# Sliding-window attention and a GELU MLP, two layers twice over: the written-out order of all queues replaced by another, with new engine choices and bank numbers

## The chip, the cores and the metric

The kernel runs on one core of a Trainium2 chip. The metric is the device time of one execution in microseconds, lower is better. The profile is one execution of the kernel before; its engines are PE (TensorE matmul, with its weight loads as PEld), DVE (VectorE), ACT (ScalarE), POOL (GpSimd) and SP (SyncE, which here issues every DMA).

## The reference

Four steps on x of shape 1 x 2048 x 512, bf16, each with a residual:

```python
x = x + _A_ref(_layernorm(x, axis=-1), A_wqkv, A_wo)
x = x + _B_ref(_layernorm(x, axis=-1), B_w1, B_b1, B_w2, B_b2)
x = x + _A_ref(_layernorm(x, axis=-1), A_wqkv, A_wo)
x = x + _B_ref(_layernorm(x, axis=-1), B_w1, B_b1, B_w2, B_b2)
```

A is attention with 32 heads of 16, each position seeing itself and the 255 positions before it, and an output projection. B is an MLP 512 to 1792 to 512 with a tanh GELU. The two layers use the same weights twice.

## The kernel before, in words

The 2048 positions are 16 tiles of 128, and the two repetitions make 32 tiles. Attention goes by blocks of two tiles: blocks 0 to 7 are the first repetition, 8 to 15 the second. The MLP goes by ten jobs of two or four tiles (jobs 0 to 9). What one repetition writes to X the next one reads, tile by tile, so that a block of the second repetition can start as soon as its tiles have left the MLP.

For each block: layernorm statistics on DVE (L591, L593), the power of -1/2 on POOL (L603, L609; L603 can also run on DVE), the normalized tile on DVE (L619), its transpose by DMA (L624), or on PE for tiles 0 to 3 of the first and the last two of the last MLP (L631, moved out of PSUM on DVE at L580 or on ACT at L582). Then the projections on PE (L645): Q moved out by DVE (L580) or ACT (L582), K by DVE with a parity mask (L679), V by DVE or ACT (L580, L582). A copy of V shifted by 64 partitions is made by two DMAs.

Scores come in "visits": ten per block, five in the first block of a repetition. One visit computes 512 columns for four head pairs into two pairs of PSUM banks (L746, 8 to 24 matmuls of 32 rows, four at a time side by side), then ACT takes the exponential of each pair of banks (L753, 128 x 1024, two per visit, 300 in all), and DVE or POOL multiplies the parts at the window's edge by a 0/1 mask (L774). After half of the visits, PE multiplies by V and a column of ones (L796, 64-row and 17-column pieces), DVE transposes the result (L805), takes the reciprocal of the sums (L809), DVE or POOL normalizes (L813), DVE transposes back (L819), PE projects (L645, Wo_sb) and DVE adds the residual (L841).

An MLP job runs 14 first products (L645, xnTB with W_sb); six of them are moved out by DVE with the bias (L863) and pass through GELU on ACT in pairs (L866), eight go straight through GELU on ACT (L871). The second product (L645, W_sb with gT) accumulates 14 matmuls per tile; POOL prepares X + b2 in advance (L879), DVE adds (L886), and in the second repetition SP writes the tile out (L890). The last tile's second product is done in two halves of 256 columns.

**What sets the order.** Every step is a node: a PE step (one to 128 matmuls), one instruction of DVE, ACT or POOL, or one DMA. There are 3097. Nothing is scheduled when the program is built: `_ORDER` is a list of all node numbers, and each engine executes its nodes in the order in which they stand there. `_ALT` lists the nodes that run on their second engine instead of their first, and `_BANKS` gives, in that same order, the first PSUM bank of each group that is opened. A recording layer (`_Sched.op`) then adds the semaphore waits that the data and the eight banks require.

```python
for i in _ALT:
    nodes[i]["eng"], nodes[i]["fn"] = nodes[i]["alts"][1]
...
for i in _ORDER:
    ...
    for g, k in nd["alloc"]:
        b = next(banks)
        gmap[g] = tuple(range(b, b + k))
```

PE has 18 warm-up matmuls on a tile of zeros (L531; seven of them with 32 columns instead of 512), which stand at the start of its queue, and one small transpose of the MLP's bias (L564), whose input comes by a DMA of its own.

Of the kernel before, what the change touches and what calls it, by code (L numbers as in the profile page):

```python
# [19 lines left out]
class _Sched:  # L20
# [147 lines left out]
    15, 34, 5, 0, 6, 14, 35, 7, 33, 28, 38, 29, 47, 8, 18, 23, 9, 36, 3, 26, 31, 10, 57, 37, 11, 22, 1, 40, 4, 24, 2,  # L168
    58, 59, 61, 17, 42, 62, 21, 60, 65, 41, 63, 19, 64, 68, 55, 32, 66, 107, 39, 69, 67, 20, 105, 50, 70, 48, 30, 27,
    53, 25, 106, 108, 71, 109, 49, 72, 110, 73, 16, 74, 114, 81, 75, 82, 111, 83, 84, 115, 85, 86, 116, 112, 87, 88,  # L170
    89, 113, 195, 153, 117, 127, 128, 151, 196, 129, 130, 154, 118, 152, 131, 119, 197, 155, 120, 156, 98, 99, 100,
    121, 12, 101, 90, 13, 102, 367, 91, 368, 104, 159, 92, 93, 157, 94, 103, 325, 76, 369, 199, 77, 326, 95, 78, 200,
    79, 370, 132, 80, 133, 96, 134, 135, 201, 323, 97, 203, 198, 137, 136, 158, 138, 205, 144, 139, 202, 140, 145,
    204, 141, 146, 160, 147, 122, 520, 217, 148, 123, 206, 124, 219, 143, 125, 208, 126, 46, 218, 324, 43, 213, 209,
    327, 328, 215, 166, 167, 168, 331, 169, 214, 207, 371, 176, 329, 177, 521, 373, 210, 178, 330, 216, 179, 522, 171,
    172, 180, 372, 161, 173, 211, 142, 174, 170, 56, 375, 220, 162, 376, 332, 163, 164, 523, 175, 524, 221, 374, 377,
    150, 212, 165, 149, 380, 378, 222, 188, 382, 189, 44, 190, 181, 45, 525, 182, 381, 223, 385, 183, 224, 191, 386,
    184, 384, 226, 225, 227, 54, 231, 232, 387, 379, 233, 526, 234, 383, 333, 228, 185, 343, 388, 389, 334, 192, 229,
    235, 344, 395, 194, 230, 335, 396, 345, 238, 346, 291, 390, 236, 397, 239, 237, 347, 240, 336, 241, 348, 337, 349,
    338, 242, 350, 244, 339, 243, 391, 399, 351, 401, 340, 341, 352, 400, 245, 403, 342, 392, 402, 51, 353, 405, 52,  # L180
    354, 355, 398, 356, 186, 360, 404, 357, 361, 362, 527, 363, 393, 408, 364, 253, 409, 260, 261, 407, 254, 262, 410,
    359, 413, 255, 246, 247, 415, 411, 256, 412, 257, 248, 249, 250, 258, 414, 406, 564, 251, 273, 394, 274, 566, 263,
    276, 416, 267, 268, 417, 565, 264, 270, 271, 265, 277, 642, 285, 286, 423, 567, 418, 640, 275, 643, 528, 287, 529,
    428, 272, 419, 282, 252, 283, 429, 288, 259, 289, 641, 420, 308, 290, 309, 421, 424, 266, 310, 311, 279, 278, 644,
    269, 422, 645, 284, 307, 280, 312, 281, 313, 314, 315, 540, 425, 426, 568, 427, 541, 570, 316, 648, 542, 543, 649,
    317, 569, 544, 318, 530, 531, 319, 532, 187, 533, 572, 534, 193, 320, 574, 321, 646, 430, 431, 322, 647, 292, 573,
    293, 294, 432, 577, 295, 435, 579, 366, 576, 296, 545, 297, 436, 358, 571, 298, 433, 578, 546, 582, 434, 547, 437,
    584, 548, 575, 550, 438, 899, 551, 552, 650, 583, 553, 439, 651, 441, 652, 440, 653, 554, 900, 897, 585, 592, 654,
    299, 549, 300, 301, 593, 365, 302, 303, 304, 442, 581, 305, 594, 586, 535, 536, 898, 580, 596, 537, 306, 598, 538,
    587, 901, 539, 902, 597, 595, 600, 588, 557, 601, 660, 661, 662, 663, 599, 602, 605, 664, 558, 559, 607, 560, 655,  # L190
    656, 561, 457, 458, 606, 603, 610, 903, 657, 589, 658, 612, 904, 604, 453, 590, 459, 454, 476, 455, 477, 611, 485,
    486, 563, 609, 479, 591, 480, 482, 562, 613, 659, 470, 471, 483, 556, 905, 464, 465, 467, 478, 468, 484, 608, 450,
    460, 469, 461, 906, 451, 466, 446, 452, 447, 481, 443, 487, 448, 444, 473, 472, 462, 665, 474, 456, 614, 666, 667,
    445, 463, 615, 449, 475, 616, 684, 625, 626, 668, 617, 489, 686, 620, 618, 490, 491, 492, 685, 493, 619, 621, 494,
    669, 688, 687, 627, 690, 628, 622, 629, 495, 488, 623, 689, 496, 632, 692, 497, 694, 498, 624, 691, 499, 500, 501,
    630, 502, 693, 697, 504, 631, 505, 633, 1017, 506, 698, 507, 508, 634, 509, 1018, 510, 503, 635, 699, 511, 702,
    1019, 670, 512, 704, 700, 671, 672, 1020, 695, 673, 1021, 703, 674, 712, 696, 513, 514, 701, 676, 714, 515, 706,
    516, 517, 705, 518, 713, 519, 716, 638, 707, 717, 715, 718, 833, 720, 708, 721, 677, 917, 1022, 918, 919, 709,
    722, 920, 719, 710, 725, 921, 678, 727, 679, 680, 724, 681, 726, 730, 922, 636, 923, 1023, 731, 912, 924, 728,
    1024, 913, 723, 914, 915, 732, 729, 925, 711, 941, 637, 943, 734, 907, 908, 909, 733, 910, 916, 926, 555, 735,  # L200
    942, 639, 1025, 911, 736, 945, 934, 946, 935, 675, 737, 947, 738, 683, 949, 1026, 936, 739, 948, 951, 937, 740,
    938, 741, 742, 682, 950, 743, 944, 954, 744, 745, 955, 746, 747, 750, 952, 748, 940, 927, 749, 956, 959, 953, 928,
    752, 929, 961, 930, 1037, 751, 1038, 753, 931, 1039, 754, 1040, 960, 755, 957, 969, 970, 756, 758, 757, 963, 971,
    973, 962, 1027, 1028, 1041, 974, 1029, 759, 1030, 1031, 958, 977, 978, 964, 975, 787, 965, 788, 979, 789, 976,
    790, 776, 782, 791, 982, 981, 777, 1274, 983, 778, 779, 972, 780, 984, 987, 980, 783, 784, 988, 785, 966, 986,
    765, 786, 766, 767, 985, 768, 989, 771, 769, 772, 773, 774, 991, 1061, 775, 1063, 990, 1065, 967, 1067, 992, 968,
    1062, 1276, 760, 761, 762, 1066, 993, 763, 803, 804, 805, 806, 1068, 1277, 764, 1069, 798, 1070, 994, 799, 800,
    1275, 995, 801, 818, 1071, 819, 820, 821, 1278, 808, 996, 849, 809, 810, 811, 793, 997, 1279, 998, 999, 770, 794,
    1064, 1000, 823, 1001, 795, 807, 796, 1002, 1072, 824, 797, 825, 826, 1003, 781, 1004, 1005, 828, 1006, 829, 792,
    1032, 1033, 1007, 830, 834, 1034, 822, 1282, 831, 835, 1009, 1035, 812, 836, 1280, 837, 802, 813, 1010, 814, 1281,  # L210
    1396, 815, 827, 816, 838, 1073, 839, 1008, 817, 1394, 840, 1283, 841, 842, 832, 1011, 843, 1012, 844, 845, 1074,
    933, 846, 847, 850, 848, 851, 1075, 932, 852, 853, 1015, 854, 881, 855, 1036, 1076, 856, 1079, 1395, 1397, 857,
    1080, 858, 1078, 1077, 859, 860, 882, 861, 1081, 1089, 862, 863, 1090, 883, 1083, 1082, 884, 885, 864, 886, 1091,
# [742 lines left out]
```

## Time and profile before

| what | value |
|---|---|
| median of three runs | 442.81 us (441.93 to 443.56) |
| the profiled execution's own time | 441.99 us |
| its span | 440.2 us |
| PE busy | 423.4 us, 96% |
| ACT busy | 386.1 us, 88% |
| DVE busy | 340.6 us, 77% |
| POOL busy | 212.7 us, 48% |

The span is the time from the first to the last instruction that the profiler saw; about 1.8 us lie around it. A busy share is an average over the whole span: it doesn't say which engine holds up the others at a given time. For that one reads the waits and the windows, stretch by stretch.

### The profile page before, as it was taken

The page shows a single profiled execution, that of the slowest core. Times are in us where ns is not written, and L with a number is a line of the kernel's source. Part 1 is how long each engine was busy: PE and PEld are TensorE (multiplying, and loading weights), DVE is VectorE, ACT ScalarE, POOL GpSimd, SP SyncE. Part 2 cuts the span into 40 slices and gives each one's busy share as a digit, 9 for nine tenths or more (in the row PEclk, how much of TensorE's full clock was granted, in tenths as well). Part 3 has the DMA queues.
Part 4 walks back from the last instruction along what each step waited for, and adds up shares of the span by engine and source line. Part 5 has one row for each costly group of instructions (what it writes and reads, how often), then busy time and mean ns, then how long its engine had stood idle before and what let it go on. Part 6 is the DMA issues. An engine that isn't in the chain of part 4 may idle for free.

```text
span 440.2 us, 16933 instructions
## 1 busy us (share of the span) xinstructions
PE 423.4 (96%) x7593; PEld 232.0 (53%) x7593; DVE 340.6 (77%) x638; ACT 386.1 (88%) x457; POOL 212.7 (48%) x236
## 2 busy tenths in 40 slices
PE   8998999988799998999999999999999999999997
PEld 4555657544444454554454455464555464444675
DVE  7998798888776599966798878867887576746762
ACT  4998999999989999889898989998897988999533
POOL 3466445363452584712566354724728165804411
DMA  7697422004101013021031021100321014003002
GB/s 232 189 179 219 87 63 45 20 10 74 35 3 38 3 34 68 17 46 25 3 70 26 1 58 25 42 14 11 67 39 20 20 39 105 14 1 85 12 0 73
DMA packets 48117, 23.25 MB, mean 53 GB/s; under 512 B 33197, under 2 KB 48045, under 8 KB 48045
## 3 DMA queue, kind: packets, MB, share of 16 engines
q1 hardware_dynamic: 48044, 22.17, 22.3%
q8 instruction: 60, 0.98, 0.9%
q14 instruction: 13, 0.10, 0.1%
HBM read 8.00 MB, written 2.10 MB: 23 GB/s over the span
## 4 chain that ended last, share of the span: by engine, by line
PE 86%; ACT 7%; DVE 3%; DMA 1%; issue 1%; SPq 1%; POOL 0%
PE ps L645 67%; PE ps L746 10%; PE ps L796 9%; ACT E L753 7%; DMA Wqkv_sb<-in_A_wqkv_dram 1%; DVE OD L805 1%; DVE E L774 0%; ACT QT L582 0%; DVE gT L863 0%; DVE stat L591 0%; DVE X L841 0%; SPq L540 0%; POOL Nb L813 0%; SPq L545 0%; DVE OT L819 0%
## 5 line engine op out<-in xcount | busy, mean ns | idle before, releaser
L753 ACT ACTIVATE E<-ps 128x1024 bf16<-128x1024 f32 x300 | 284.0, 1034 | 26.0 <-PE ps L746 25.1
L774 POOL TENSOR_TENSOR E<-E,mask 128x512 bf16<-128x512 bf16 (+2 forms) x111 | 120.9, 1106 | 89.5 <-ACT E L753 89.5
L645 PE MATMUL ps<-W_sb,gT 128*128 128x512 bf16 (+1 forms) x462 | 118.0, 374 | 0.2 <-DVE OD L805 0.2
L645 PE MATMUL ps<-xnTB,W_sb 128*128 128x512 bf16 (+1 forms) x560 | 111.7, 337 | 0.6 <-ACT E L753 0.5
L645 PEld LDWEIGHTS ps<-xnTB,W_sb 128*128 128x128 bf16 x560 | 51.7, 98 | 41.9 <-issue 2.7
L645 PE MATMUL ps<-xnTA,Wqkv_sb 128*128 128x256 bf16 x512 | 70.7, 273 | 0.5 <-DMA Wqkv_sb<-in_A_wqkv_dram 0.2
L774 DVE TENSOR_TENSOR E<-E,mask 128x512 bf16<-128x512 bf16 (+2 forms) x125 | 59.8, 498 | 13.4 <-ACT E L753 13.0
L746 PE MATMUL ps<-QT,KT 32*128 32x128 bf16 (+3 forms) x1920 | 60.0, 231 | 8.6 <-ACT E L753 5.2
L645 PEld LDWEIGHTS ps<-W_sb,gT 128*128 128x128 bf16 x462 | 41.1, 98 | 41.1 <-issue 3.9
L746 PEld LDWEIGHTS ps<-QT,KT 32*128 32x128 bf16 x1920 | 28.4, 92 | 58.5 <-ACT E L753 35.5
L645 PEld LDWEIGHTS ps<-xnTA,Wqkv_sb 128*128 128x128 bf16 x512 | 47.5, 98 | 20.4 <-issue 2.3
L805 DVE STREAM_TRANSPOSE OD<-ps 128x1024 f32<-128x1024 f32 x32 | 39.8, 1245 | 20.3 <-PE ps L796 19.7
L879 POOL TENSOR_TENSOR Xb<-X,b2all 128x512 f32<-128x512 bf16 x32 | 37.7, 1180 | 34.3 <-DVE X L886 33.9
L871 ACT ACTIVATE gT<-ps,b1T 128x512 bf16<-128x512 f32 (+1 forms) x80 | 42.6, 609 | 9.3 <-PE ps L645 9.2
L796 PE MATMUL ps<-E,Va 64*17 64x128 bf16 (+3 forms) x1920 | 43.3, 230 | 1.8 <-issue 0.8
L813 POOL TENSOR_TENSOR Nb<-OD,Rc 128x512 bf16<-128x512 f32 x25 | 26.4, 1057 | 38.1 <-DVE Rc L809 29.2
L796 PE MATMUL ps<-E,Vs 64*17 64x128 bf16 (+3 forms) x1920 | 44.0, 230 | 0.0
L591 DVE BATCH_NORM_STATS2 stat<-X 128x6 f32<-128x512 bf16 x64 | 42.9, 677 | 0.7 <-DMA X<-in_A_x_dram 0.3
L796 PEld LDWEIGHTS ps<-E,Va 64*17 64x17 bf16 x1920 | 36.8, 84 | 11.6 <-issue 9.0
L679 DVE TENSOR_TENSOR KT<-ps,parmask 128x1024 bf16<-128x1024 f32 x32 | 38.6, 1208 | 3.6 <-PE ps L645 3.6
L863 DVE TENSOR_SCALAR gT<-ps,b1T 128x512 bf16<-128x512 f32 (+1 forms) x60 | 36.7, 631 | 5.7 <-PE ps L645 5.3
L796 PEld LDWEIGHTS ps<-E,Vs 64*17 64x17 bf16 x1920 | 37.5, 84 | 0.1
(53 smaller groups left out, 353.4 us busy)
## 6 DMA issues: line engine op xcount, KB each, us to landing
Vs<-Va SPq DMA_DIRECT2D x64, 68.0 KB, 2.0
W_sb<-in_B_w_dram SPq DMA_DIRECT2D x4, 512.0 KB, 4.7
out_dram<-X SPq DMA_DIRECT2D x15, 128.0 KB, 1.9
X<-in_A_x_dram SPq DMA_DIRECT2D x3, 512.0 KB, 6.8
Wqkv_sb<-in_A_wqkv_dram SPq DMA_DIRECT2D x4, 256.0 KB, 5.0
W_sb<-in_B_w_dram SPq DMA_DIRECT2D x2, 384.0 KB, 7.1
W_sb<-in_B_w_dram SPq DMA_DIRECT2D x1, 768.0 KB, 5.7
Wqkv_sb<-in_A_wqkv_dram SPq DMA_DIRECT2D x1, 512.0 KB, 7.7
```

The costliest lines, as they stand in the source:

```text
L591: add("dve", lambda e, B, t=t, k6=k6: e.bn_stats(stat6[:, k6, :], X[:, t, :]), reads=["X%d" % t], writes=["st%d" % k6], key="bs%d" % (k + j))
L645: r = e.matmul(ps[:, B[g][0], cols], lhsT, rhs, start=st, stop=sp)
L679: add("dve", lambda e, B, g=g, i=i: e.tensor_tensor(out=KT[:, kb, 2 * i : 2 * i + 2].rearrange("p c m a q -> p a (c m) q"), in0=ps[:, B[g] ...
L746: x = e.matmul(ps[:, bk[r], o : o + n], KT[rows, kb, c, m].rearrange("p a q -> p (a q)"), QT[rows, c, q : q + n], start=True, stop=True)
L753: add("act", lambda e, B, g_=g_, gi=gi: e.activation(E[:, 2 * gi : 2 * gi + 2, e0 : e0 + 512], ps[:, B[g_][0] : B[g_][0] + 2, :], AF.Exp, ...
L774: fn = lambda e, B: e.tensor_tensor(out=Ew, in0=Ew, in1=Mw, op=ALU.mult)
L796: x = e.matmul(ps[32 * r : 32 * r + VW, B[g][par], c % 2 * 2 * P + lo : c % 2 * 2 * P + hi], V[rows, (2 * b + m // 2) % VR, c * HC + 2 * r ...
L805: add("dve", lambda e, B: e.transpose(OD[:, s].rearrange("p a c q -> p (a c q)"), ps[:, B[g][0] : B[g][0] + 2, :]), reads=["ps:" + g], wri ...
L813: return e.tensor_tensor(out=Nb[:, s, :].rearrange("p (k a d) -> p a k d", a=2, d=Dh), in0=sums[:, :, :, 0:Dh], in1=rc[:, :, :, None].to_b ...
L863: add("dve", lambda e, B, g=g, fc=fc: e.tensor_scalar(out=gT[:, fc, c0 : c0 + M], in0=ps[:, B[g][0], 0:M], scalar1=b1T[:, fc : fc + 1], sc ...
L871: add("act", lambda e, B, g=g, fc=fc: e.activation(gT[:, fc, c0 : c0 + M], ps[:, B[g][0], 0:M], AF.Gelu_apprx_tanh, bias=b1T[:, fc : fc + ...
L879: add("pool", lambda e, B, t=t, xs=xs: e.tensor_tensor(out=Xb[:, xs, :], in0=X[:, t, :], in1=b2all[:], op=ALU.add), reads=["X%d" % t, "b2a ...
```

## The change

Only the three lists change: `_ORDER` (all 3097 numbers stand there again, in another order), `_ALT` (172 numbers before, 171 after) and `_BANKS` (658 numbers in both). No node, shape or DMA is added or removed. Every instruction of the changed kernel exists in the kernel before too; it can stand at another place of its queue, on another engine (where it has two) and on another PSUM bank.

```diff
 _ORDER = [
-    15, 34, 5, 0, 6, 14, 35, 7, 33, 28, 38, 29, 47, 8, 18, 23, 9, 36, 3, 26, 31, 10, 57, 37, 11, 22, 1, 40, 4, 24, 2,
...
 _ALT = [
-    67, 70, 75, 102, 109, 116, 121, 148, 165, 170, 185, 192, 198, 202, 211, 216, 337, 342, 370, 374, 378, 384,
...
+    67, 70, 75, 102, 109, 116, 121, 148, 165, 170, 185, 192, 202, 207, 211, 216, 337, 370, 374, 378, 384, 389,
...
 _BANKS = [
...
-    4, 3, 6, 1, 3, 6, 4, 7, 1, 2, 5, 7,
+    2, 6, 0, 4, 1, 2, 3, 1, 2, 7, 5, 3,
```

By engine, the new lists do this:

| nodes | DVE to POOL | POOL to DVE | DVE to ACT | ACT to DVE |
|---|---|---|---|---|
| mask products (L774) | 41 | 48 | | |
| normalization (L813) | 0 | 4 | | |
| variance plus epsilon (L603) | 8 | 9 | | |
| Q out of PSUM (L580, L582) | | | 7 | 1 |
| V out of PSUM (L580, L582) | | | 3 | 2 |
| transposed tiles out of PSUM (L580, L582) | | | 2 | 0 |

By shape, the mask products on DVE go from 19, 59 and 47 (of 256, 512 and 768 columns) to 23, 57 and 52, and on POOL from 37, 57 and 17 to 33, 59 and 12. The functions on ACT come in 19 runs of one kind in both orders: the square roots of the first two tiles, then exponential and GELU in turn.

In the large the two orders run alike: of the PE work ahead of the first scores of each block, the largest difference is 0.5 us. In the small, most queues are reordered. At the start, POOL's first steps go from column numbers (L512), ones for ident (L503), ones for Va (L528), mask (L517) to mask (L517, L520), ident (L503), column numbers (L512), Va (L528); on PE the bias transpose (L564) comes ahead of the first transposes (L631) instead of behind them; and of SP's loads, the last quarter of x goes from the tenth place to the 42nd. At the end, the MLP's last job starts behind two more matmuls of the job before, and its second products are interleaved differently.

359 rows, old and new, of tables (_ALT, _BANKS, _ORDER) are left out of this document.

## The prediction

> **What bounds the kernel now.** The page comes first: three of its slice rows and its chain.
>
> ```profile
> PE   8998999988799998999999999999999999999997
> DVE  7998798888776599966798878867887576746762
> ACT  4998999999989999889898989998897988999533
> ...
> PE 86%; ACT 7%; DVE 3%; DMA 1%; issue 1%; SPq 1%; POOL 0%
> ```
>
> A slice is 11 us. PE stands at 9 nearly everywhere, but ACT too, until the last three slices; the chain goes over PE for 86% and over ACT for 7%. A 9 only says 90% or more, so the windows view cuts the span where PE's row changes character. Its columns are the length, then the busy time of PE, PEld, DVE, ACT and POOL.
>
> ```profile
> 0.00:20.00 20.00, 17.82 (x169) 10.34 (x173) 17.36 (x38) 13.92 (x19) 9.01 (x22) 1.00 0.77 224
> 20.00:215.00 195.00, 183.61 (x3670) 103.68 (x3666) 156.80 (x303) 182.31 (x216) 95.16 (x101) 1.00 0.26 55
> 215.00:400.00 185.00, 184.80 (x3226) 93.51 (x3227) 143.66 (x252) 169.68 (x193) 96.85 (x103) 1.00 0.16 34
> 400.00:440.20 40.20, 37.16 (x538) 24.43 (x536) 22.73 (x47) 20.20 (x33) 11.65 (x12) 1.00 0.14 41
> ```
>
> PE idles 2.2 us in the first 20 us, 195.00 - 183.61 = 11.4 us from 20 to 215, 0.2 us from 215 to 400 and 3.0 us at the end. ACT idles 195.00 - 182.31 = 12.7 us from 20 to 215 and 185.00 - 169.68 = 15.3 us from 215 to 400. So there are two regimes. Up to 215 us PE and ACT are both nearly full and neither is full: they wait for each other. After 215 us PE is full; a new order can't take anything out there, only put something in. PE's work itself is the same in both kernels, matmul for matmul. **What can be won lies between 20 and 215 us, and is at most some 11 us.**
>
> The waits view of that stretch says who waits for whom (total, times, longest):
>
> ```profile
> PEld ps L746 <- ACT E L753: 20.2, 43, 1.6
> ACT E L753 <- PE ps L746: 10.8, 19, 1.2
> ```
>
> PE's score matmuls wait for banks that an exponential has yet to empty, 43 times, and ACT's exponentials wait for scores 19 times. The waits of weight loads (PEld) are longer than PE's idle time, since a load waits while the matmul before it still runs. This is a circle between two in-order queues: how many other matmuls stand between one visit's scores and the next decides whether it closes early or late.
>
> **The change, part by part.** No instruction is new, so every duration is in this trace; groups with the shapes kept apart (count, then busy us, mean ns):
>
> ```profile
> L774 POOL TENSOR_TENSOR E<-E,mask 128x512 bf16<-128x512 bf16 x57 | 66.1, 1167 | 52.6 <-ACT E L753 52.6
> L774 DVE TENSOR_TENSOR E<-E,mask 128x512 bf16<-128x512 bf16 x59 | 29.3, 508 | 4.8 <-ACT E L753 4.6
> L774 POOL TENSOR_TENSOR E<-E,mask 128x768 bf16<-128x768 bf16 x17 | 29.9, 1762 | 11.2 <-ACT E L753 11.2
> L774 DVE TENSOR_TENSOR E<-E,mask 128x768 bf16<-128x768 bf16 x47 | 26.1, 573 | 8.3 <-ACT E L753 8.2
> L774 POOL TENSOR_TENSOR E<-E,mask 128x256 bf16<-128x256 bf16 x37 | 26.1, 709 | 25.8 <-ACT E L753 25.8
> L774 DVE TENSOR_TENSOR E<-E,mask 128x256 bf16<-128x256 bf16 x19 | 5.4, 283 | 0.3 <-ACT E L753 0.2
> L813 POOL TENSOR_TENSOR Nb<-OD,Rc 128x512 bf16<-128x512 f32 x25 | 26.4, 1057 | 38.1 <-DVE Rc L809 29.2 <-DVE statmv L593 8.9
> L813 DVE TENSOR_TENSOR Nb<-OD,Rc 128x512 bf16<-128x512 f32 x7 | 5.1, 735 | 0.2
> L580 DVE CAST QT<-ps 128x512 bf16<-128x512 f32 x19 | 13.0, 682 | 6.7 <-PE ps L645 6.5
> L582 ACT ACTIVATE QT<-ps 128x512 bf16<-128x512 f32 x13 | 8.0, 615 | 2.9 <-PE ps L645 2.9
> L580 DVE CAST Va<-ps 128x512 bf16<-128x512 f32 x22 | 14.9, 676 | 3.1 <-PE ps L645 3.0
> L582 ACT ACTIVATE Va<-ps 128x512 bf16<-128x512 f32 x10 | 6.1, 625 | 1.0 <-PE ps L645 0.9
> L582 ACT ACTIVATE xnTA<-ps 128x512 bf16<-128x512 bf16 x3 | 1.7, 595 | 1.4 <-PE ps L631 1.4
> L580 DVE COPY xnTB<-ps 128x512 bf16<-128x512 bf16 x2 | 0.8, 420 | 1.0 <-PE ps L631 1.0
> ```
>
> *Engine loads.* ACT gets a net six Q, one V and two transposed tiles: 6 x 0.615 + 0.625 + 2 x 0.595 = +5.5 us. DVE loses these, 6 x 0.682 + 0.676 + 2 x 0.420 = -5.6 us, and takes masks (4 x 0.283 - 2 x 0.508 + 5 x 0.573 = +3.0 us) and four normalizations (4 x 0.735 = +2.9 us): +0.3 us net. POOL loses 4 x 0.709 - 2 x 1.167 + 5 x 1.762 = 9.3 us of masks and 4 x 1.057 = 4.2 us of normalizations. One L603 more on DVE and one less on POOL are some 0.2 us each. POOL is half idle, so its 13.5 us are worth only the earlier ends of single masks: a 768-column mask ends 1762 - 573 = 1.2 us sooner on DVE. ACT's 5.5 us lie thus by blocks: net +0.6 us in blocks 3 to 8, +3.7 us in blocks 9 to 15 (four Q, two V), +1.2 us at the end. The 3.7 us fall where ACT idles 15.3 us beside a full PE: **nothing**, as long as they don't stand in front of an exponential that PE is waiting for; uncovered they cost up to 3.7 us. The table loads of ACT stay, since its functions come in 19 runs in both orders.
>
> *The order between 20 and 215 us.* For every group of banks that ACT frees I counted, in both orders, the PE work between the scores (or product) that ACT has to read and the matmul that reuses its bank. The units are these groups:
>
> ```profile
> L645 PE MATMUL ps<-W_sb,gT 128*128 128x512 bf16 x434 | 114.3, 380 | 0.2 <-DVE OD L805 0.2
> L753 ACT ACTIVATE E<-ps 128x1024 bf16<-128x1024 f32 x300 | 284.0, 1034 | 26.0 <-PE ps L746 25.1
> ```
>
> The places themselves are rows of the timeline (start, length; in brackets the idle time before it and what ended it):
>
> ```profile
> 40.19 0.40 PE L746 MATMUL ps<-QT,KT 32*128 32x192 bf16 x12 [0.96 <-ACT E L753]
> ...
> 113.75 0.40 PE L746 MATMUL ps<-QT,KT 32*128 32x256 bf16 x8 [1.30 <-ACT E L753]
> ...
> 200.51 2.10 PE L645 MATMUL ps<-W_sb,gT 128*128 128x512 bf16 x9
> ```
>
> Nine matmuls take 2.10 us, of which the last one's own 0.38 us is latency: (2.10 - 0.38) / 8 = 0.215 us each. An exponential takes 1.03 us, so with less than 1.3 us (six matmuls) ahead of it a score visit may well wait. The row at 113.75 is the worst place: in block 4, visit 6 stood directly behind visit 5, with no matmul between, and PE idled 1.30 us. In the new order two matmuls stand there (+0.43 us of cover). The row at 40.19 (block 1, visit 7) goes from 0.66 to 1.09 us of cover. Most other stalls of the stretch have the same neighbours in both orders; of those that change, visit 9 of block 3 gets 0.43 us more, visit 9 of block 4 0.2 us, visit 7 of block 7 0.43 us, and visit 2 of block 4 loses 0.2 us. Together 0.43 + 0.43 + 0.43 + 0.2 + 0.43 - 0.2 = 1.7 us to the good. Against it stand new short places: over the whole kernel 69 groups that ACT frees have under 1.3 us of cover before and 70 after, 71 and 71 of those that DVE frees. So the new order has as many short places, at other spots, and I take back 0.7 us: **-1.0 us**. Bounds: all of PE's idle time gone, -11.4 us; and, if each of the 43 waits came 0.14 us later (a quarter of the 0.615 us of a Q ahead of it), +6 us.
>
> *From 215 to 400 us.* PE is full, cover under 1.3 us grows by a few groups here, and ACT is fuller: **+0.3 us**, between 0 and 3.7 us.
>
> *The start.* These rows are POOL's, DVE's and PE's first steps:
>
> ```profile
> 0.89 0.13 POOL L512 IOTA pidx<- 128x2 int32 x1 [0.40 <-POOLq L941]
> ...
> 0.96 0.20 POOL L503 MEMSET ident<- 128x128 bf16 x1
> ...
> 1.10 1.45 POOL L528 MEMSET Va<- 128x320 bf16 x1
> 1.36 1.37 DVE L513 TENSOR_SCALAR pidx<-pidx 128x2 int32<-128x2 int32 x1
> ...
> 2.15 0.56 POOL L517 MEMSET mask<- 128x192 bf16 x1
> 2.77 0.17 DVE L515 TENSOR_SCALAR parmask<-pidx 128x2 f32<-128x2 int32 x1
> ...
> 2.94 0.69 DVE L591 BATCH_NORM_STATS2 stat<-X 128x6 f32<-128x512 bf16 x1
> ...
> 9.59 0.28 PE L645 MATMUL ps<-xnTA,Wqkv_sb 128*128 128x256 bf16 x1 [0.18 <-DMA Wqkv_sb<-in_A_wqkv_dram]
> ```
>
> The first statistics stand behind L513 and L515 on DVE. POOL now makes the mask (0.56 us and a first cut of it), and ident (0.20 us) before the column numbers (0.13 us), which come at about 0.9 + 0.56 + 0.2 + 0.2 + 0.13 = 2.0 us instead of 1.0; L513 with its 1.37 us and L515 follow, and the statistics start near 3.7 instead of 2.94, +0.8 us. On PE the bias transpose moves ahead of the first transposes, behind warm-ups that fill the time. But the row at 9.59 shows that PE's second K product waits for a weight DMA, whose place on SP's queue stays: most of the lateness ends there. What is left is K's move out of PSUM, half a microsecond later on DVE: **+0.3 us**, between 0 and +0.8. [...]
>
> *The end.*
>
> ```profile
> L871 ACT ACTIVATE gT<-ps,b1T 128x256 bf16<-128x256 f32 x32 | 12.8, 480 | 9.2 <-PE ps L645 9.2
> ...
> 430.78 1.93 ACT L871 ACTIVATE gT<-ps,b1T 128x256 bf16<-128x256 f32 x5
> ...
> 437.20 0.69 DVE L886 TENSOR_TENSOR X<-Xb,ps 128x512 bf16<-128x512 f32 x1 [2.20 <-PE ps L645]
> ```
>
> The last sum and its DMA are the same. The last job's GELUs now begin behind its matmul pair 10 of 28, by the PE work that follows 9.8 us before PE ends. Eleven steps at (1.93 - 0.48) / 4 = 0.36 us, three of them some 0.15 us longer, are 4.4 us, and waits for the last bias adds on DVE 1.1 us: they end 4.3 us before PE does. The last matmul that reads them first starts 3.6 us before the end: cover 0.7 us, so **0**, and up to +1 us where it fails. The two transposed tiles are ready on ACT about as late as PE wants them.
>
> **The sum.** 0.3 - 1.0 + 0.3 + 0 = -0.4 us on the profiled execution's own 441.99 us. That run lies 0.8 us under the median of 442.81 us; on the median the sum gives **442.4 us**, which I forecast.
>
> **Rivals.** (1) *The circle opens*: most of the long waits between 20 and 215 us go, not just those I counted. For it: PE idles 11.4 us there and ACT 12.7 us, so both queues have room, and five of the six stalls that change get more cover. Against it: as many short covers as before. If half of the idle time goes, 442.8 - 5.7 = 437.1 us. (2) *ACT's new work closes it*: the nine operations stand in front of exponentials that PE waits for, in queue order, so PE waits too. Place: Q and V of blocks 3 to 15; price: all of 5.5 us, 442.8 + 5.5 = 448.3 us. It decides once 2.6 us of them are uncovered, for 2.6 - 0.4 is 2.2 us, half a per cent. For it: ACT's idle time is waits for scores, not free room, and PE is full after 215 us, so that whatever PE waits there is lost. Against it: a Q moved out on ACT (615 ns) comes no later than on DVE (682 ns), whose queue gets shorter at that spot. (3) *The reordering does nothing*: PE's idle time moves elsewhere, 442.8 us; it lies inside the forecast's own range.
>
> **How the numbers follow.** Half a per cent, 2.2 us, is what a measurement here can tell from no change. Forecast with rival 3, 440.6 to 445.0: 0.36. Rival 1, under 440.6: 0.31. Rival 2, over 445.0: 0.33, since many small places can be worse at once and only one stretch can be better. The range reaches to both rivals' prices and a little over, leaving a tenth on either side: 436.5 to 449.5.
>
> **What would show it.** Right: PE's idle time from 20 to 215 us near 10 us, under 1 us from 215 to 400, the stalls in block 4 at visit 6 shorter, the first exponential about 0.3 us later than 11.35 us, ACT busy near 391 us. Rival 1: that idle time at 6 us or less. Rival 2: PE idle by some microseconds after 215 us, ended by ACT. Wrong altogether: a wait for a mask, a DMA transpose or POOL among PE's longest.

## The result, and the profile after

| | before | after |
|---|---|---|
| median (range; runs) | 442.58 us (441.93 to 443.56; 7) | 444.27 us (443.31 to 444.80; 7) |
| ratio, 95% interval | | 1.0035 [1.0023, 1.0048] |
| profiled execution, its span | 441.99, 440.2 us | 444.5, 442.6 us |

The change costs 1.7 us where 0.4 us less was forecast. A second set of runs of the same two kernels gave 444.62 beside 442.65 us, 1.0040 [1.0027, 1.0052].

From the page of the kernel after: busy time by engine, PE's slices, the code transfers of the DMA queue table, and the chain.

```profile
PE 416.2 (94%) x7523; PEld 232.4 (53%) x7593; DVE 340.5 (77%) x641; ACT 390.8 (88%) x466; POOL 200.4 (45%) x224
PE   8988999988889997999999999999999999999997
q8 instruction: 60, 0.98, 0.9%
PE 72%; ACT 17%; DVE 7%; issue 2%; DMA 1%; POOL 0%; DVEq 0%; SPq 0%
```

ACT is busy 390.8 us, as worked out (386.1 + 5.5 = 391.6). PE's busy time can't be compared: PE did 7593 matmuls (PEld has them all), and 70 of their records are missing, each of which looks like 0.2 us of idle time ended by "issue". The chain tells more: PE's share fell from 86% to 72%, ACT's rose from 7 to 17 and DVE's from 3 to 7.

PE's rows of the waits view (total, times, longest), 20 to 215 us: two of the kernel before, then four of the kernel after, then one of the kernel after from 215 to 400 us:

```profile
PE ps L746 <- ACT E L753: 5.0, 8, 1.3
PE ps L796 <- issue: 0.8, 2, 0.6
```

```profile
PE ps L746 <- ACT E L753: 3.4, 8, 0.9
PE ps L645 <- issue: 1.6, 10, 0.2
PE ps L796 <- issue: 1.5, 2, 1.0
PE ps L746 <- DVE OD L805: 1.3, 1, 1.3
```

```profile
PE ps L796 <- DMA xnTB<-xn: 0.5, 1, 0.5
```

PE's waits for exponentials shrink from 5.0 to 3.4 us, as wanted. Two things are new: a product with V that stands 1.0 us and waits for no semaphore (a wait of 0.5 to 0.6 us of this kind, in block 3, is in both kernels), and one in block 14 that stands 0.5 us behind a DMA transpose. The row of L645 behind "issue" is the missing records.

**Where the time goes.** Because of the missing records I took the start of every PE step, less the PE work ahead of it, each kind of step at one fixed length in all kernels. This lateness grows only where PE stands. The first column counts PE work, not time: 12 us of work are done some 14 us into the span, 204 us at some 231. In us, from two profiles of each kernel (the second ones are from the runs before_again and after_again below):

| PE work done | before | before, 2nd | after | after, 2nd | growth, after less before |
|---|---|---|---|---|---|
| 12 | 1.96 | 1.99 | 1.98 | 2.06 | 0.0 |
| 60 | 7.78 | 8.09 | 8.79 | 8.77 | +0.8 |
| 72 | 8.30 | 8.60 | 10.36 | 10.14 | +0.95 |
| 204 | 26.52 | 27.03 | 28.23 | 28.14 | -0.4 |
| 336 | 32.18 | 32.77 | 34.13 | 34.12 | +0.25 |
| 348 | 32.86 | 33.46 | 35.32 | 35.34 | +0.5 |
| 396 | 34.13 | 34.74 | 36.59 | 36.61 | 0.0 |

The last column is the difference of the two means since the row above. Nearly all of the 2.2 us arises at three places.

*Block 1, 33 to 44 us, +0.8 us.* The chain of the kernel after (start, length, what):

```profile
38.32 1.16 DVE OD L805
39.48 1.11 DVE KT L679
40.59 0.61 DVE QT L580
41.20 0.05 issue
41.25 1.69 PE ps L645 x7
```

Block 3's second half of Q moved from ACT to DVE, where it stands behind a K move; V's product behind it wants its bank. Just ahead of that, V of tile 5 leaves PSUM on ACT behind two exponentials (at 37.31 us; in the kernel before at 33.32), and the next score visit needs its banks and stands 0.41 us by the waits view (0.57 us if counted from the end of the work ahead of it, as in the expectation below).

*Block 2's first product with V, +0.95 us.* The chain of the kernel after, then one row of the kernel before:

```profile
68.26 1.14 PE ps L796 x98
69.40 0.96 issue
70.36 0.43 PE ps L796 x21
```

```profile
67.52 1.38 PE ps L796 x122
```

The product stands in its middle, with all inputs there. "Issue" means that nothing in the profile released it.

*Block 14's first product with V, +0.5 us.* The chain of the kernel after:

```profile
371.41 2.44 DMA xnTB<-xn
373.85 0.04 issue
373.90 1.51 PE ps L796 x121
```

The mask product that it needs stands on DVE behind a normalized tile that waits for its buffer's DMA transpose; in the kernel before it ran ahead of that tile.

**A theory for the second place.** The page has 60 "instruction" transfers of 0.98 MB / 60 = 16 KB, and PE executes 7593 weight loads and as many matmuls: 253 of them per transfer, or 15342 / 60 = 255.7 with the 156 semaphore waits and drains of PE's queue in the trace. I call 256 instructions a piece, and the moment at which PE starts a new piece a crossing. The instruction that stands is number 2243 = 9 x 256 - 61 in PE's program, a boundary of that grid (its offset, the 61, is an estimate that fits the crossings; no row shows it). In both orders, the transfer that a crossing sets off usually starts 0.05 to 1 us later and takes 0.9 to 1.6 us; I read it as bringing the piece behind the next boundary, which in this profile runs 1.35 us after the transfer's end (1.2 to 1.4 us where PE stands for it in the profiles below). So two crossings should lie some 0.9 + 1.0 + 1.35 = 3.25 us apart (an estimate from these figures), and a product with V runs through a whole piece in 1.4 us. Here the transfer started only at 68.07 us, 2.36 us after its crossing at 65.71: two DMA transposes (packets at 65.88 to 66.80 and 67.18 to 68.11) went first. The rival: the stall belongs to this product's data or banks. The runs below measure how far each holds.

### The profile page after: what moved, and what is told of

It reads as the page before. It is cut to its first block, busy times and chain, and to the rows that moved or that the text cites. A ratio compares the mean times of both kernels' runs of the same rounds, so it can differ in the third digit from the quotient of the medians.

```text
span 442.6 us, 16842 instructions
## 1 busy us (share of the span) xinstructions
PE 416.2 (94%) x7523; PEld 232.4 (53%) x7593; DVE 340.5 (77%) x641; ACT 390.8 (88%) x466; POOL 200.4 (45%) x224
## 4 chain that ended last, share of the span: by engine, by line
PE 72%; ACT 17%; DVE 7%; issue 2%; DMA 1%; POOL 0%; DVEq 0%; SPq 0%
PE ps L645 55%; ACT E L753 15%; PE ps L796 8%; PE ps L746 8%; DVE OD L805 1%; DVE stat L591 1%; PE ps L531 1%; DVE X L841 1%; DVE gT L863 1%; ACT L753 1%; ACT QT L582 1%; DMA xnTB<-xn 1%; DVE Va L580 1%; DVE E L774 1%; DVE KT L679 1%
## 5 line engine op out<-in xcount | busy, mean ns | idle before, releaser
L774 POOL TENSOR_TENSOR E<-E,mask 128x512 bf16<-128x512 bf16 (+2 forms) x104 | 112.9, 1098 | 97.2 <-ACT E L753 97.1
L645 PE MATMUL ps<-W_sb,gT 128*128 128x512 bf16 (+1 forms) x434 | 110.5, 373 | 3.0 <-issue 2.5
L645 PE MATMUL ps<-xnTB,W_sb 128*128 128x512 bf16 (+1 forms) x540 | 107.4, 335 | 2.9 <-issue 1.3
L645 PEld LDWEIGHTS ps<-xnTB,W_sb 128*128 128x128 bf16 x560 | 51.6, 98 | 41.0 <-issue 3.2
L645 PE MATMUL ps<-xnTA,Wqkv_sb 128*128 128x256 bf16 x512 | 70.7, 273 | 1.1 <-ACT xnTA L582 0.4
L774 DVE TENSOR_TENSOR E<-E,mask 128x512 bf16<-128x512 bf16 (+2 forms) x132 | 61.9, 493 | 5.8 <-ACT E L753 5.4
L645 PEld LDWEIGHTS ps<-W_sb,gT 128*128 128x128 bf16 x462 | 40.9, 98 | 41.2 <-issue 3.4
L645 PEld LDWEIGHTS ps<-xnTA,Wqkv_sb 128*128 128x128 bf16 x512 | 47.1, 98 | 20.8 <-issue 2.8
L805 DVE STREAM_TRANSPOSE OD<-ps 128x1024 f32<-128x1024 f32 x32 | 39.9, 1246 | 18.5 <-PE ps L796 18.4
L813 POOL TENSOR_TENSOR Nb<-OD,Rc 128x512 bf16<-128x512 f32 x21 | 22.4, 1065 | 47.5 <-DVE Rc L809 32.3
L886 DVE TENSOR_TENSOR X<-Xb,ps 128x512 bf16<-128x512 f32 (+1 forms) x33 | 21.9, 665 | 28.5 <-PE ps L645 27.9
```

The lines of the kernel that those rows point to most:

```text
L645: r = e.matmul(ps[:, B[g][0], cols], lhsT, rhs, start=st, stop=sp)
L774: fn = lambda e, B: e.tensor_tensor(out=Ew, in0=Ew, in1=Mw, op=ALU.mult)
L805: add("dve", lambda e, B: e.transpose(OD[:, s].rearrange("p a c q -> p (a c q)"), ps[:, B[g][0] : B[g][0] + 2, :]), reads=["ps:" + g], wri ...
L813: return e.tensor_tensor(out=Nb[:, s, :].rearrange("p (k a d) -> p a k d", a=2, d=Dh), in0=sums[:, :, :, 0:Dh], in1=rc[:, :, :, None].to_b ...
```

## The experiments

Each ratio is to the kernel before, with its 95% interval. The interval of one repair is some 0.4% wide (1.8 us), more than its gain, so a repair is judged by the lateness in its profile, and the times say only whether the sum closes. The diffs of `_ORDER` and `_ALT` show only the stretch of numbers that changes, against the kernel after unless said otherwise.

**The first place.**

```diff
-390, 396, 236, 239, 237, 347, 397, 240, 348, 241, 349, 350, 192, 242
+390, 192, 396, 236, 239, 237, 347, 397, 240, 348, 241, 349, 350, 242
...
 _ALT
-337, 370
+337, 342, 370
```

> The changed kernel with V of tile 5 moved out of PSUM on ACT ahead of block 1's exponentials of visit 5 instead of behind them, and the second half of block 3's Q moved out on ACT instead of DVE, both as in the kernel before. Theory (two of the lost 2.4 us come from these two places in the queues): PE's stall ahead of block 1's visit 6 (0.57 us) goes, V of tile 6 and 7 start at least 0.4 us earlier, PE is 0.7 to 0.9 us earlier from 52 us on; 443.5 us beside 444.3 for the changed kernel. Rival (PE and ACT wait for each other here, and what one place gives the next one takes): PE at 60 us no earlier than in the changed kernel by more than 0.2 us; 444.2 us.

443.93 us, 1.0047 [1.0027, 1.0067]. Its chain:

```profile
39.47 1.11 DVE KT L679
40.58 0.27 DVE Rc L809
40.85 0.02 issue
40.86 1.67 PE ps L645 x7
```

V's product starts at 40.86 instead of 41.25, and from 12 to 60 us of work PE's lateness grows by 6.18 us instead of 6.76: 0.6 us of the 0.8 come back, a little under the 0.7 to 0.9 expected. The stall in block 2 was missing in this execution (transfer 0.10 us after the crossing).

**The second place, transposes earlier.**

```diff
-575, 549, 550, 551, 552, 553, 583, 650, 651, 439, 652, 441, 653
+575, 550, 551, 552, 553, 583, 650, 651, 439, 652, 441, 549, 653
```

> The changed kernel with one DVE step moved: block 4's K leaves PSUM behind the two normalized tiles 34 and 35 (MLP job 1) instead of ahead of them, so that their two DMA transposes are issued 1.1 us or more earlier, near 63.5 us instead of 64.70. Theory (PE's 0.96 us without a semaphore in block 2's product with V, at its 98th matmul, is PE waiting for its own next 16 KB of code, whose DMA starts only when the packets of those two transposes are through, 2.36 us after PE crossed the boundary before): that stall is under 0.2 us, the code transfer starts within 1.6 us of the crossing, and PE is 0.8 to 1.1 us earlier from 71 us on; 443.3 us. Rival (the stall belongs to this product with V, through its data or its banks): it stays at 0.9 to 1.2 us, 444.3 us.

444.30 us, 1.0055 [1.0035, 1.0075]. The transfer starts 0.15 us after the crossing and the stall is gone, though the product and its data are the same, which speaks against the rival. The transposes came only 0.42 us earlier (64.28), and the gain didn't stay: K leaves its bank later, Q's next product comes 0.45 us late for it, and two score visits behind it come 0.42 and 0.32 us late, ended by moves on DVE (L805, L580) in the waits view. Of 1.1 us, 0.1 were left at 84 us of work (12.04 beside 12.17), no more than two profiles of one kernel differ by.

**The third place.**

```diff
-2801, 2781, 2362, 2626, 2380, 2803, 2363, 2791,
+2801, 2781, 2362, 2791, 2626, 2380, 2803, 2363,
```

> The changed kernel with one DVE step moved: the mask product of block 14, visit 4, second pair, goes ahead of the normalized tile 59 (which waits for its buffer's DMA transpose), as in the kernel before. Theory: PE's stall ahead of block 14's first product with V (0.5 to 0.6 us near 373.9) goes and nothing takes its place, as PE is full here; 443.75 us. Rival (the product waits for POOL's or ACT's last piece of E just as late): 444.3 us, the stall stays.

443.79 us, 1.0045 [1.0024, 1.0066]. Its chain at this place:

```profile
371.90 1.03 PE ps L645 x4
372.93 1.60 PE ps L796 x120
```

The product follows the matmuls ahead of it. From 336 to 348 us of work, lateness grows by 0.80 us instead of 1.2: 0.4 us back, of 0.5.

**Moving the boundaries.**

```diff
-            add("pe", lambda e, B, g="w%d" % h, n=32 if h in WSHORT else 512: e.matmul(
-                ps[:, B[g][0], 0:n], gT[:, 0, 0:P], gT[:, 0, 0:n], start=True, stop=True),
+            def warm(e, B, g="w%d" % h, h=h):
+                n = 32 if h in WSHORT else 512
+                c = n // CUT if n == 512 else n
+                for i in range(CUT if n == 512 else REP.get(h, 1)):
+                    lo = c * i if n == 512 else 0
+                    r = e.matmul(ps[:, B[g][0], lo : lo + c], gT[:, 0, 0:P], gT[:, 0, lo : lo + c], start=True, stop=True)
+                return r
+            add("pe", warm,
```

CUT is 4 and REP empty in shift66 and before_shift66; in shift256 CUT is 8 and the seven short warm-ups run 8, 8, 8, 8, 8, 8 and 10 times.

> The changed kernel with each of the 11 long warm-up matmuls (512 columns of zeros) cut into four of 128 columns: the same columns, 33 more matmuls and their weight loads, so that all later PE instructions stand 66 places further in PE's program; nothing else changes. Theory (PE's program comes in pieces of 256 instructions, and PE stalls where two boundaries are less than about 3.25 us apart): with the boundaries moved by 66 places, the crossing times of the changed kernel's trace give some 14 pairs that are too close, 14.6 us of stalls in all if none overlaps another; the transfers of the warm-ups cost nothing. 452 to 460 us, best guess 457, with PE's longest idle times ended by no semaphore and inside products with V. Rival (code fetch is hidden, the stall in block 2 has another cause): 444.0 to 444.8 us.

455.79 us, 1.0313 [1.0290, 1.0336]: 11.5 us slower than the changed kernel, for 33 warm-up matmuls of the same columns. (The expectation's 14.6 us was a misreading, as the next expectation says; the same working for the way the boundaries were moved, done after the result, gives 11.1.) Two places of its chain, with its lines 9 higher:

```profile
35.10 1.31 PE ps L805 x112
36.41 1.96 issue
38.37 0.27 PE ps L805 x7
```

```profile
240.86 0.27 PE ps L755 x5
241.13 1.78 issue
242.91 0.32 PE ps L755 x4
```

From the crossing times of the changed kernel, that working has 1.79 us at 36.5 us in block 1's first product with V, and 1.80 us in block 9's visit 7 at 234.7 us, which the stalls before it move to 241. The old stall in block 2 is gone. The stalls of over 0.25 us in its chain sum to 10.7 us.

> The changed kernel with the warm-up matmuls cut finer still: 128 more of them, so that all later PE instructions stand 256 places further, exactly one piece of code, and every boundary falls on the same instruction as in the changed kernel. Theory (it is the place of the boundaries that cost 11.5 us in the shift by 66, not the cut warm-ups): 444.3 us as the changed kernel, at most 0.6 us more or less, with one transfer of code more. Rival (more and smaller matmuls at the start are the cost, through PE's clock, the loads or the instructions themselves): 455 us or more, since four times as many are added. Of the shift by 66, this belongs to its record: the 14.6 us of its expectation were read off for boundaries moved by 66 places the other way; the same working for the way they were moved gives 11.1 us.

446.10 us, 1.0074 [1.0051, 1.0096]. PE's waits without a releaser from 20 to 440 us, a row of the timeline at the start, and the first exponentials in the chain, of this kernel; then the first exponentials of the changed one:

```profile
PE ps L654 <- issue: 5.6, 35, 0.2
PE ps L805 <- issue: 0.5, 1, 0.5
```

```profile
10.31 1.05 PE L654 MATMUL ps<-xnTA,Wqkv_sb 128*128 128x256 bf16 x8 [0.99 <-DMA Wqkv_sb<-in_A_wqkv_dram]
```

```profile
13.53 1.94 ACT E L762 x2
```

```profile
11.64 1.94 ACT E L753 x2
```

The first row is missing records; the second is the wait of 0.5 us in block 3 that the changed kernel and the kernel before have too. So from 20 us on no boundary costs anything. The 1.8 us over the changed kernel arise at the start, where everything comes 1.89 us later: the finer warm-ups take 0.7 us more before the first projection (8.27 instead of 7.55 us), and then PE stands 0.99 us for a load of Wqkv that was there in time in the changed kernel. The added code transfer runs from 7.21 to 8.77 us, beside the loads; whether it holds them up is not shown. So a shift by 256 costs at most this, and one by 66 costs 11.5 us: the cost is in where the boundaries fall. Block 2's stall is missing here too.

> The kernel before with its long warm-up matmuls cut in four, as in the shift of the changed kernel by 66 places. Theory (PE stalls where two boundaries are under 3.25 us apart, whatever the order): the crossing times of its own trace give 10.9 us, so 453.3 us, 451 to 456. Rival (the order before is robust against the place of the boundaries, and the changed one lost its time to that): 442 to 446 us.

460.48 us, 1.0405 [1.0380, 1.0431]: the order before is as sensitive. The sum 10.9 us was too small by 7: the stall in block 1 is 3.57 us instead of 1.39, and the granted clock falls to half behind three of the long stalls (more on that below).

**Three more ways to clear the second place.** In the first (the diff), the normalized tiles 34 and 35 and their transposes move behind five DVE steps (its expectation says four). The second is the same with the edits of v5_q3 and mask_first, the two repairs, and the third has those too and puts the tiles behind three mask products more (440, 442, 439 and 441 behind 580).

```diff
-583, 650, 651, 439, 652, 441, 653, 440, 581, 592, 654, 900, 554, 535, 536, 594, 537, 897, 538, 442, 299, 300, 539, 898, 301
+583, 650, 651, 652, 653, 581, 592, 654, 900, 554, 535, 536, 594, 537, 897, 538, 299, 300, 539, 898, 439, 441, 440, 442, 301
```

> The changed kernel with the normalized tiles 34 and 35 and their two DMA transposes moved later on DVE and SP (by four DVE steps, 64.23 to some 66 us), so that PE's code transfer comes first and block 4's K stays where it is. In the run that moved them earlier, the stall without a semaphore went, but K's bank opened 0.45 us later and the gain was gone by 78 us. Theory (the transposes in flight hold up the transfer of code): the transfer starts within 1 us of PE's crossing at 65.7 us, the stall is under 0.2 us, PE is 0.7 to 1.1 us earlier from 76 us on; 443.4 us. Rival (PE and ACT are in a circle here, and ACT's exponentials take back whatever PE gains): the stall goes, PE is less than 0.3 us earlier at 78 us; 444.2 us.

> The changed kernel with the three repairs at once: V of tile 5 and block 3's Q on ACT as in the kernel before, the normalized tiles 34 and 35 later, the mask of block 14 ahead of normalized tile 59. Theory (the three places are the loss): 0.65 + 1.0 + 0.45 = 2.1 us off the changed kernel's 444.3, so 442.2 us, level with the kernel before within 0.5 us. Rival (there are many more places, and repairs in the stretch up to 215 us don't add): 443.3 us or more.

> The three repairs at once again, with the normalized tiles 34 and 35 three mask products later still, so that their transposes are issued near 67 us, 2 us after PE crosses the boundary at 65.2, instead of 0.65 us after it. (In the run before they came just ahead of the code transfer, which then started 3.94 us after the crossing; PE stood for 2.5 us and its granted clock was half for 4 us after.) Theory: the transfer starts within 1.3 us of the crossing, no stall over 0.3 us there, the other two places as in their own runs; 442.2 us, level with the kernel before within 0.5 us. Rival (other places take it back): 443.3 us or more.

xn_late: 444.38 us, 1.0045 [1.0028, 1.0061]; no stall at the place, but in the profiled execution PE had stood 2.2 us for a transpose in block 2's projections, so it met the transposes at another time. all_three: 444.03 us, 1.0034 [1.0015, 1.0053]; the stall was 2.48 us in the profile, whose execution (447.85 us) was the slowest of its twelve. three_apart: 444.22 us, 1.0048 [1.0025, 1.0072]; no stall, but MLP job 1 waited 0.8 us for its tiles. The 442.2 us that the last two were to reach came in neither.

> The changed kernel itself, once more, beside the repairs on the same chip: 444.3 us, 443.3 to 444.8 as in its first runs. Its stall without a semaphore in block 2 depends on whether the code transfer or the two transposes come first, so it may be missing or longer in some executions, which would show as a spread of 2 us or more.

444.62 us, 1.0040 [1.0027, 1.0052], 443.08 to 444.93. The stall is there again (0.90 us), the mask's too; the expected spread isn't.

The next kernel has the two repairs alone.

> The changed kernel with the two repairs that each worked alone (V of tile 5 and block 3's Q on ACT as before; block 14's mask ahead of normalized tile 59), nothing about the two transposes. Theory: 0.65 + 0.45 us less, 443.2 to 443.5 us beside 444.3 to 444.6 for the changed kernel; in its profile PE ahead of the changed kernel by 0.5 to 0.8 us at 60 us and by 0.9 to 1.3 us at 390 us. The stall in block 2 may or may not show in the one profiled execution. Rival (no gain beyond the spread): 444.3 us.

445.06 us, 1.0052 [1.0027, 1.0078]: no gain. (One of its twelve executions took 818 us; the record doesn't show why, and the median is the same without it.) Block 1 does gain (lateness 8.54 instead of 8.77 to 8.79 at 60 us, although here job 0 stood 0.5 us for its transposed tiles), and block 14 too, but the stall in block 2 is now 2.06 us by the chain.

The two repairs, and tile 35 with its transpose alone later:

```diff
-652, 441, 653, 440, 581, 592, 654, 900, 554, 535, 536, 594, 537, 897, 538, 442, 299, 300, 539, 898, 301, 586, 596
+652, 653, 440, 581, 592, 654, 900, 554, 535, 536, 594, 537, 897, 538, 299, 300, 539, 898, 301, 586, 441, 442, 596
```

> The two repairs, and of the two normalized tiles only the second one (35) later, behind one mask product, so that its DMA transpose is issued near 66.7 us instead of directly behind that of tile 34. Theory: between the two transposes the code transfer gets through and starts within 1.6 us of PE's crossing at 65.3 us, no stall over 0.3 us in block 2's first product with V; the MLP's job 1 finds tile 35 transposed by 71 us and does not wait for it (it did, by 0.8 us, when both came at 67.8). 442.3 us, level with the kernel before within 0.5 us, and without the changed kernel's runs of 446 us and more. Rival (any later transpose makes job 1 wait, or other places take the gain): 443.2 us or more.

444.19 us, 1.0043 [1.0025, 1.0062]; stall 1.85 us. The code transfer did not use the 1.5 us between the two transposes.

The packets' records of these profiles, in us:

| kernel | PE crosses | transposes' packets | code starts | PE stands |
|---|---|---|---|---|
| before | 64.97 | 64.74-65.66, 67.68-68.60 | 65.55 | 0 |
| before, 2nd | 65.28 | 65.05-65.94, 67.93-68.84 | 65.87 | 0 |
| after | 65.71 | 65.88-66.80, 67.18-68.11 | 68.07 | 1.17 |
| after, 2nd | 65.76 | 65.93-66.84, 67.23-68.15 | 67.94 | 0.90 |
| mask_first | 65.38 | 65.55-66.45, 66.85-67.74 | 67.66 | 1.17 |
| v5_q3 | 65.29 | 65.46-67.75, 67.96-68.80 | 65.39 | 0 |
| two_repairs | 65.19 | 65.36-66.28, 66.67-67.59 | 68.61 | 2.28 |
| split_transposes | 65.24 | 65.41-66.33, 67.81-68.72 | 68.56 | 2.07 |
| xn_first | 66.17 | 65.45-66.37, 66.77-68.18 | 66.32 | 0 |
| all_three | 65.20 | 67.02-67.94, 68.33-69.18 | 69.14 | 2.70 |
| three_apart | 65.83 | 68.93-69.85, 70.25-72.60 | 65.88 | 0 |
| two_and_mid | 65.03 | 67.33-68.25, 68.65-69.57 | 65.14 | 0 |

(The last column is the whole gap between the two matmuls; the chain takes the first matmul's own time off it.) The code either starts at once, or at the end of the first transpose if the crossing falls into it, or only after both. It isn't for want of free DMA engines: in all_three no packet moved for the first 1.8 us after the crossing, and the code still came behind both transposes, which were issued 0.65 us after the crossing; in two_repairs it came 1.0 us after them, behind a copy of V too. What decides the order is not shown. In the new order the crossing falls 0.17 us ahead of the first packets, and it can go either way: v5_q3 and two_repairs have the same spacing and opposite outcomes.

> The kernel before itself, once more, for a second profile: 442.6 us. Theory: its PE stands where it stood in the first profile within 0.5 us at 60, 200 and 390 us, so that the 2.4 us found between one profile of each kernel are the change's and not the execution's. Rival (the first profile, 0.7 us under the median of its kernel's runs, was a lucky execution in blocks 1 and 2): PE is later by 0.6 us or more from some place in the first 80 us on.

442.51 us, 0.9992 [0.9981, 1.0002]. Later by 0.3 us at 60 us of work and 0.6 us at 396: the rival's size, though not from one place. Half of that 0.6, 0.3 us, is what the means of the table take off the 2.4 us between the first two profiles. The expectation's 0.5 us was a little narrow.

**Between too early and too late**, with the two repairs:

```diff
-439, 652, 441, 653, 440, 581, 592, 654, 900, 554, 535, 536, 594, 537, 897, 538, 442, 299, 300, 539, 898, 301, 586
+652, 653, 581, 592, 654, 900, 554, 535, 536, 594, 537, 897, 538, 299, 300, 539, 898, 301, 586, 439, 441, 440, 442
```

> The changed kernel with the two repairs, and both normalized tiles 34 and 35 behind one mask product, so that their transposes are issued near 66.5 us: 1.2 us after PE's crossing at 65.3 us (0.65 us was too close in the run all_three; at 67.8 us, in three_apart, MLP job 1 waited 0.8 us for them). Theory: code transfer within 1 us of the crossing, no stall over 0.3 us in block 2's first product with V, job 1 waits 0.3 us at most; profile within 0.6 us of the kernel before's second profile at 80 us and later; 442.6 us, and a spread of about 1.5 us like that of the kernel before instead of 4 us and more. Rival (the spread and the loss come from elsewhere): 443.8 us or more with runs over 446 us.

443.39 us, 1.0024 [1.0009, 1.0039]. Its chain at the place:

```profile
66.61 0.97 PE ps L645 x4
67.58 1.67 PE ps L796 x121
69.24 0.02 issue
69.27 1.26 DVE OD L805
```

No stall, no wait of job 1. Lateness at 396 us of work is 34.56, beside 34.13 and 34.74 before and 36.6 after; its span of 440.6 us lies between those of the kernel before (440.2 and 440.8). So in the profiled execution the three places are the whole difference. It was the fastest of its twelve (442.54 us), though. The median gives back 0.9 to 1.2 of the 1.7 to 2.0 us, and its interval overlaps that of the kernel after; single executions still reach 445.6 and 449.5 us, and what they meet stays open.

**The kernel before, loads moved.** One, then three of the loads of W2 (L570) go later on SP's queue.

```diff
-227, 54, 231
+227, 231
...
-405, 52, 354
+405, 52, 54, 354
```

That is the first; in the second 51, 52 and 54 stand together behind 359.

> The kernel before with one weight load moved (the last quarter of W2, not needed before some 60 us, goes behind the second and third transposes on SP's queue instead of ahead of V's shifted copy at 31 us). In the kernel before the code transfer after PE's crossing at 35.55 us starts 2.08 us later, while the weight loads run at 340 to 400 GB/s, and block 1's visit 7 starts at 40.19, 0.65 us after its inputs. Theory (loads hold up code as transposes do): the transfer starts at least 0.6 us earlier, visit 7 follows its inputs within 0.2 us, PE is 0.4 to 0.6 us earlier at 45 us; 442.0 us beside 442.5. Rival (the transfer isn't what visit 7 waits for, or ACT takes the gain back): PE at 45 us within 0.2 us of the kernel before; 442.5 us.

> The kernel before with three of the four loads of W2 moved behind V's shifted copies of tile 6 (near 45 us; W2 is needed from some 58 us on). In the kernel before one of them holds up the code transfer at 35.55 us, and two share the DMA engines with the transposes of job 0's tiles, whose first product stands 0.35 to 0.65 us. Theory: visit 7 of block 1 starts 0.4 us earlier, the first product of job 0 doesn't wait, PE is 0.5 to 1.0 us earlier at 55 us; 441.8 us beside 442.55. Rival (ACT's exponentials set the pace here, and take it back): 442.5 us. Danger: the loads meet the code transfer at 49.6 us; then a stall shows in block 1's second product with V.

442.58 us, 1.0005 [0.9993, 1.0017], and 442.53 us, 1.0005 [0.9990, 1.0020]: nothing. Visit 7 started at 39.80 and 39.84 us instead of 40.19, but so it did in before_again (39.82), where nothing was moved; that 0.4 us was the first execution's. In all three of these profiles, before_again's too, the code transfer at this place starts at 36.29 to 36.32 us instead of 37.63, so the loads aren't shown to hold it up. In the first one visit 7 starts 1.44 us after that transfer's end (38.75 us), about as PE does behind the stalls above; that it waited for code there is likely, not shown. Job 0's first product came 0.4 to 0.8 us later than in the first profile, 0.1 to 0.4 us later than in before_again. No version beat the kernel before.

## Why the prediction was wrong, point by point

- **The start, +0.3 us.** The first exponential came at 11.64 us instead of 11.35, the 0.3 us that was worked out, but in part by luck. The statistics came at 3.23 us, 0.3 us later and not 0.8, PE's second K product didn't wait for its weights (9.53 us), and the first scores start at 10.79 us in both kernels. ACT's rows, before and after:

```profile
9.44 0.60 ACT L582 ACTIVATE xnTA<-ps 128x512 bf16<-128x512 bf16 x1 [0.50 <-PE ps L631]
10.06 1.28 ACT L753 ACT_TABLE_LOAD   x1
```

```profile
9.73 0.60 ACT L582 ACTIVATE xnTA<-ps 128x512 bf16<-128x512 bf16 x1 [0.50 <-PE ps L631]
10.35 1.28 ACT L753 ACT_TABLE_LOAD   x1
```

  The exponential follows the table load, which stands behind a transposed tile. For PE the term was mis-sized: at 12 us of work it is level with the kernel before (1.98 and 2.06 beside 1.96 and 1.99), so the term is 0.
- **20 to 215 us, -1.0 us.** This is the step that failed: +0.8 + 0.95 - 0.4 = +1.35 us (12 to 204 us of work), inside its bounds and with the wrong sign. Most of the counted gains are there: block 4's visit 6 now has this row of the timeline, and from 72 to 204 us of work the new order gains 0.4 us.

```profile
115.49 0.40 PE L746 MATMUL ps<-QT,KT 32*128 32x256 bf16 x8 [0.89 <-ACT E L753]
```

  It stood 1.30 us before and stands 0.89 now, 0.41 less for 0.43 of new cover. Visit 9 of block 3 stands 0.15 us instead of 0.60, visit 7 of block 7 0.12 instead of 0.40. Visit 7 of block 1 gained nothing clear (0.85 us, beside 0.96 and 0.78 in the two profiles before), and block 7's first product with V now stands 0.57 us (0.26 in the second profile). What failed is the claim that counting cover covers the stretch: against 1.7 us of gains the sum set 0.7 us for new short places, and two places alone cost 1.75 us. I counted PE work between a score and the reuse of its bank; I didn't ask where a move out of PSUM stands in its own engine's queue. V of tile 5 had cover, but behind two exponentials on ACT; Q had it, but behind a K move on DVE. And a stall that no semaphore ends wasn't among my terms at all. The upper bound was loose too: of its 43 waits of weight loads, only 8 stopped PE itself (5.0 us).
- **215 to 400 us, +0.3 us.** Measured +0.75: 0.5 from one mask product, the rest spread. The bounds held. The cause was another: not ACT's added work, but a mask behind a step that waits for a DMA, which the text had listed under "wrong altogether".
- **The end, 0.** Measured 0.0 from 348 us of work on.
- **ACT's load**, 391 us: 390.8.
- **Rival 2** (ACT's added work closes the circle) named the right sign, not the mechanism: ACT's nine more operations aren't where the time goes, and one of the two moved steps in block 1 had gone from ACT to DVE. Rival 1's five better covers gained 0.4 us of its 5.7. Rival 3 (PE's idle time moves elsewhere) is nearest: the result lies in the band, 440.6 to 445.0 us, that it shared with the forecast, but 1.7 us on the slow side and clear of no change.

## What to carry to other kernels

Ahead of a reordering, walk each moved step along its own queue: what now stands ahead of it there, and does that wait for anything? One mask behind one step that waits for a DMA cost here as much as all the covers gained. And where PE runs many small matmuls, lay its program's 16 KB pieces over the timeline: two boundaries under some 3.3 us apart (the estimate above), or DMA transposes issued just at a crossing, went here with stalls of up to 3.6 us that no dependency shows, and 66 instructions at the front moved all the boundaries.

## What the runs showed of the hardware

- **Code fetch.** 33 more warm-ups cost 11.5 us in one order and 18 in the other; 128 more (one whole piece) cost 1.8 us, all of it at the start. By the estimate above PE stands where two crossings lie under about 3.25 us apart; in shift66 that working gave 1.79 and 1.80 us at two places where 1.96 and 1.78 us were measured, in before_shift66 1.39 us where it was 3.57. In a product with V a piece lasts 1.4 us.
- **The clock behind a stall.** The windows of all_three (PE, PEld, DVE, ACT, POOL, then the granted clock) and of two_repairs:

```profile
69.00:71.50 2.50, 0.02 (x5) 0.01 (x4) 0.00 (x0) 0.28 (x1) 0.80 (x1) 0.87 0.16 37
71.50:72.00 0.50, 0.50 (x21) 0.21 (x21) 0.00 (x0) 0.00 (x0) 0.00 (x0) 0.50 0.00 0
74.00:75.00 1.00, 0.78 (x4) 0.29 (x2) 0.51 (x1) 0.63 (x1) 1.00 (x2) 0.50 0.00 0
```

```profile
68.00:71.00 3.00, 0.94 (x107) 0.80 (x92) 0.79 (x2) 1.27 (x2) 1.46 (x2) 1.00 0.11 27
71.00:72.00 1.00, 1.00 (x37) 0.67 (x38) 0.59 (x1) 0.27 (x1) 0.00 (x0) 1.00 0.00 0
```

  After a stall of 2.48 us the clock is half until 77.6 us, some 6 us long (not the 4 us of three_apart's expectation); after one of 2.06 us it stays at 1.00. In shift66 stalls of 1.78 and 1.96 us were followed by about 3 us of half a clock and one of 2.04 us was not. So a stall of about 2 us can cost another 1.5 to 3 us (an estimate: half of the 3 to 6 us), and its length alone doesn't decide; what else does is not shown.
